# First batch of packed attention with a two-layer MoE: order of loads, weight conversion and products

## Chip, cores and metric

One core of a Trainium2 chip runs the whole program. The metric is device microseconds of one execution. The engines are named PE (TensorE, matrix products; PEld is its weight load), DVE (VectorE), ACT (ScalarE), POOL (GpSimd) and SP (SyncE, which issues all DMAs here).

## The reference, cut to what matters

```python
batch, n_heads, seq, head_dim = (8, 8, 576, 64); n_pack = 32
def sm_attn(qq, kk, vv):
    s = scale * np.matmul(qq, kk.transpose(0, 1, 3, 2))
    s = s - np.max(s, axis=-1, keepdims=True)
    a = np.exp(s)
    a = a / (np.sum(a, axis=-1, keepdims=True) + 1e-09)
    return np.matmul(a, vv)
p_packed = sm_attn(p, k, v)
out = sm_attn(q, p_packed, p_packed)
x = out, heads side by side            # 4608 tokens x 512
h = x @ w_in;  g = np.maximum(0.01 * h, h);  x = g @ w_out        # first layer, d_ff 2048
h = x @ w_in2; g = h / (1 + np.exp(-1.702 * h)); out = g @ w_out2 # second layer
```

The attention inputs are single precision. The four weights come as double precision, and the kernel reads them as pairs of 32-bit words.

## The kernel before, in words

There are four stages: attention together with the first layer's input product (batch by batch, about the first quarter of the span), the first output product, the second input product, and the second output product. The change is in the first stage only, and in it in batch 0 and in the steps of batch 1 that are prepared during batch 0.

**A batch.** `s1` (L221) makes the scores of packed queries against keys, their maxima on DVE and their exponentials on ACT. `packed` (L251) transposes the exponentials on PE, copies them on ACT and DVE, multiplies by the values, scales, and leaves the packed result in `ppk` (L284). `s2` (L286) exists for two halves of 288 tokens: scores of the queries against `ppk` on PE, a 32x32 transpose on DVE (L296), maximum and difference (L299, L300), exponential on ACT (L302), sum, reciprocal and scaling (L305 to L308), transpose back (L313), a rounded high part on ACT (L315) and the low part on DVE (L317). `prod_m` (L319) multiplies `ppk` with one chunk of 512 columns of the converted `w_in1` (four chunks c = 0 to 3), and splits the result into a high part (ACT, L325) and a low part (DVE, L327). `l1` (L331) is the main product: one unit is one block of 128 output columns for one half, six matmuls (L338), then the leaky unit on ACT (L343), which frees the PSUM bank (three such banks). A batch has 32 units; units 0 to 7 use chunk 0, 8 to 15 chunk 1, 16 to 23 chunk 2, 24 to 31 chunk 3. After each fourth call on a pair of blocks SP stores the result.

**Conversion.** `w_in1` is converted during batch 0 alone. `load_w1(c)` issues four DMAs of 512 KB (L365) into eight rotating buffers, so chunk c+2 overwrites chunk c. `w1_piece(c, k)` converts one of the four pieces of a chunk in `to_f32` (L115): two ACT operations (L121, L122), then two DVE operations (L125, L128), then one addition on POOL (L129). The scratch tile that L122 writes and L129 reads has four copies, one for each k, so chunk c+1's piece k may write it only when the addition of chunk c's piece k has ended. A product of chunk c needs all four pieces.

**Order.** Every engine executes its own instructions in program order. Up to the first unit the order is written out by hand (L377 to L404). After that, unit n is followed by `side(n)`, which issues what has been put on the agenda for that step by `at` and `pieces`; each `next` of a generator issues the work up to its next `yield`, and `run(piece, n)` does n of these. In the kernel before, chunk 0 is converted inside the first half's softmax, units 0 to 3 follow on the first half, then units 4 to 7 on the second; chunks 1, 2 and 3 are converted at steps 0 to 4, 8 to 12 and 16 to 20, each piece with ACT at one step and DVE and POOL at the next, and their products stand at steps 5, 13 and 21. Batch 1's `s1`, `packed` and the two `s2` stand at steps 8 to 12, 14 to 21, 22 to 29 and 24 to 31, its first product at 26 to 29, and batch 2's `s1` begins at step 29.

**PSUM.** Scores, transposes and products share five rotating banks under one tag (`aux`), so a late release of one holds up whatever comes five allocations later.

Of the kernel before, what the change touches and what calls it, by code (L numbers as in the profile page):

```python
# [46 lines left out]
def packed_attention_moe_moe_kernel(tc, qT, kT, vm, vt, pT, w_in1, w_out1, w_in2, w_out2, out):  # L47
# [32 lines left out]
    with ExitStack() as ctx:  # L80
# [10 lines left out]
        def at(step, *todo):  # L91
            agenda.setdefault(step, []).extend(todo)
# [16 lines left out]
        def pieces(piece, steps):  # L109

            for step in steps:
                at(step, lambda: next(piece, None))
# [73 lines left out]
        def aux(name):  # L186
            return ps.tile([P, 512], F32, tag="aux", name=name, bufs=5)

        def load_p(b):
            tp[b] = px.tile([P, H, J], F32, tag="p", name=f"p_{b}")  # L190
            nc.sync.dma_start(tp[b], pT[b])

        def load_k(b):
            tk[b] = px.tile([P, 2, 2, S], F32, tag="k", name=f"k_{b}")
            for g in range(2):
                nc.sync.dma_start(tk[b][:, g], kT[b, g])
# [7 lines left out]
        def load_q(b):  # L204
            tq[b] = px.tile([P, 2, 4, TH], F32, tag="q", name=f"q_{b}")
            for hf in range(2):
                nc.sync.dma_start(tq[b][:, hf], qT[b, hf])
# [13 lines left out]
        def s1(b):  # L221
            k, p = tk.pop(b), tp.pop(b)
            t = [[None, None], [None, None]]
            for hf in range(2):
                for par in range(2):
                    t[par][hf] = aux(f"s1_{b}_{par}_{hf}")
                both([t[0][hf], t[1][hf]], lambda r, i, par: p[r, 2 * i + par, :],
                     lambda r, i: k[r, i // 2, i % 2, hf * TH:hf * TH + TH], TH)
            if b:
                after(load_k, b + 1)  # L230
                after(load_p, b + 1)
            yield
            mx, sm = (px.tile([P, 2, 2], F32, tag=w, name=f"{w}_{b}") for w in ("mx", "sm"))
            nb, r = (px.tile([P, 2], F32, tag=w, name=f"{w}_{b}", bufs=2) for w in ("nb", "r"))
            e = px.tile([P, 2, S], F32, tag="e", name=f"e_{b}")
            e1[b] = e, r
            for par in range(2):
                for hf in range(2):
                    nc.vector.reduce_max(mx[:, par, hf:hf + 1], t[par][hf][:, :TH], axis=AX.X)
                nc.vector.tensor_scalar(nb[:, par:par + 1], mx[:, par, 0:1], mx[:, par, 1:2], -SCALE, op0=ALU.max, op1=ALU.mult)  # L240
                yield
            for par in range(2):
                for hf in range(2):
                    nc.scalar.activation(e[:, par, hf * TH:hf * TH + TH], t[par][hf][:, :TH], AF.Exp, bias=nb[:, par:par + 1],
                                         scale=SCALE, accum_out=sm[:, par, hf:hf + 1])
                yield
            for par in range(2):
                nc.vector.tensor_scalar(r[:, par:par + 1], sm[:, par, 0:1], sm[:, par, 1:2], 1e-9, op0=ALU.add, op1=ALU.add)
            nc.vector.reciprocal(r, r)

        def packed(b):  # L251

            e, r = e1.pop(b)
            et = px.tile([P, 2, 5, P], F32, tag="et", name=f"et_{b}")
            rest = aux(f"tr_{b}")
            for par in range(2):
                t = aux(f"t1_{b}_{par}")
                for k in range(4):
                    nc.tensor.transpose(t[:, P * k:P * k + P], e[:, par, P * k:P * k + P], ident)
                nc.tensor.transpose(rest[:64, P * par:P * par + P], e[:, par, 512:576], ident)  # L260
                yield
                nc.scalar.copy(et[:, par, 0:4, :], t.rearrange("p (k n) -> p k n", k=4))
            nc.vector.tensor_copy(et[:64, :, 4, :], rest[:64, :2 * P].rearrange("p (a n) -> p a n", a=2))
            yield
            v = tv.pop(b)
            o = px.tile([P, 2, D], F32, tag="o", name=f"o_{b}")
            for par in range(2):
                t = aux(f"pp_{b}_{par}")
                for k in range(5):
                    n = P if k < 4 else 64  # L270
                    for i in range(4):
                        c0 = D * (2 * (i % 2) + par)
                        nc.tensor.matmul(t[32 * i:32 * i + 32, :D], lhsT=et[:n, par, k, 32 * i:32 * i + 32],  # L273
                                         rhs=v[:n, i // 2, k, c0:c0 + D], start=(k == 0), stop=(k == 4))
                if par and b:
                    after(load_v, b + 1)
                yield
                nc.vector.tensor_scalar(o[:, par, :], t[:, :D], r[:, par:par + 1], None, op0=ALU.mult)
            yield
            t = aux(f"t2_{b}")  # L280
            nc.tensor.transpose(t[:, :P], o.rearrange("p a d -> p (a d)"), ident)
            yield
            ppk[b] = px.tile([P, 4, J], F32, tag="ppk", name=f"ppk_{b}", bufs=2)
            nc.scalar.copy(ppk[b], t[:, :P].rearrange("p (i j) -> p i j", i=4))  # L284
# [66 lines left out]
        def warm(n):  # L351

            for _ in range(n):
                nc.tensor.matmul(keep[:, :P], lhsT=ident, rhs=ident, start=True, stop=True)
# [4 lines left out]
        raw1 = {}  # L359

        def load_w1(c):
            for k in range(4):
                n = (4 * c + k) % 8
                raw1[c, k] = room[:, 1024 * n:1024 * n + 1024]
                nc.sync.dma_start(raw1[c, k], w_in1_v[:, k, 1024 * c:1024 * c + 1024])  # L365

        def w1_piece(c, k):
            v = room[:, 8192 + 512 * (k % 4):8704 + 512 * (k % 4)].bitcast(F32)
            yield from to_f32(w1[:, k, 512 * c:512 * c + 512], raw1[c, k].rearrange("p (w t) -> p w t", t=2), v)

        def run(piece, n=99):
            for _ in range(n):
                if next(piece, 0) == 0:
                    break


        load_p(0)  # L377
        load_k(0)
        load_v(0)
        load_q(0)  # L380
        load_w1(0)
        load_w1(1)
        warm(20)
        run(s1(0))
        load_k(1)
        load_p(1)
        warm(8)
        run(packed(0))
        load_v(1)
        halves = [s2(0, hf) for hf in range(2)]  # L390
        next(halves[0])
        next(halves[1])
        load_q(1)
        w1p = [w1_piece(0, k) for k in range(4)]
        next(halves[0])
        for k in range(4):
            next(w1p[k])
            if k < 3:
                next(halves[0])
            next(w1p[k])  # L400
        run(halves[0])
        m0 = prod_m(0, 0)
        run(m0)
        load_w1(2)  # L404
        pieces(halves[1], (0, 0, 0, 1, 2, 2, 3))
        at(5, lambda: load_w1(3))
        for c in range(1, 4):
            for k in range(4):
                s = 8 * c - 8 + k
                at(s, lambda c=c, k=k: raw1.update({("p", c, k): w1_piece(c, k)}))  # L410
                at(s, lambda c=c, k=k: next(raw1["p", c, k]))
                at(s + 1, lambda c=c, k=k: next(raw1["p", c, k]))
            pieces(prod_m(0, c), (8 * c - 3, 8 * c - 3, 8 * c - 2, 8 * c - 1))
        for b in range(B):
            s = 32 * b
            if b + 1 < B:
                if b == 0:
                    first, second = (8, 9, 9, 10, 11, 12), range(14, 22)
                    third, fourth = range(22, 30), range(24, 32)
                else:  # L420
                    first, second = (-3, -2, -2, 0, 1, 2), range(5, 13)
                    third, fourth = ([k + i for k in (0, 1, 2, 4, 5, 7, 10, 11)] for i in (13, 17))
                for piece, when in ((s1(b + 1), first), (packed(b + 1), second), (s2(b + 1, 0), third),
                                    (s2(b + 1, 1), fourth), (prod_m(b + 1, 0), range(26, 30))):
                    pieces(piece, [s + k for k in when])
            if b:
                for c in range(1, 4):
                    pieces(prod_m(b, c), [s + 8 * c - 6 + k for k in range(4)])
# [110 lines left out]
        for k in range(EARLY):  # L539
            s = 32 * (B - 2) + 20 + 8 * k  # L540
# [182 lines left out]
        for q in range(2):  # L723
            s = 14 * NJ * q
# [3 lines left out]
        for k in range(EARLY):  # L728
            s = 7 * (4 * NJ + 2 * k + 2)
# [82 lines left out]
```

## Time and profile before

| | |
|---|---|
| median of 3 runs | 1481.79 us (1481.16 to 1482.88) |
| the profiled execution's own time | 1488.2 us |
| its span | 1486.4 us |
| busy: PE, DVE, ACT, POOL | 95%, 75%, 56%, 7% of the span |
| mean granted PE clock | 0.98 of full speed |

The span is the time from the first to the last instruction of the profiled execution. Busy shares are means over stages with different limits. Stretches are given in microseconds from the span's start. In a list of instructions in order of time the columns are start, duration, engine, line, operation, tile written and tiles read, shapes, count, and in brackets the engine's idle time before it with what ended it. In a list of groups they are the count, the busy time and the mean of one in ns, and the idle time before with what ended it.

### The profile page before, as it was taken

Reading aid. Unit: us, or ns where it says so; the run is one execution under the profiler, and the core shown is the slowest. Engines: PE = TensorE matmul, PEld = TensorE weight load, DVE = VectorE, ACT = ScalarE, POOL = GpSimd, SP = SyncE. Lnnn points to the kernel's source line nnn. Section 1 sums busy time; section 2 is a strip of 40 time slices with the busy share of each in tenths; the row PEclk is TensorE's granted clock in tenths of the full one; section 3 lists DMA queues with packets and bytes.
Section 4 is the critical chain, followed back from the end, with each engine's and each line's share of the span. In section 5 each row is a group of like instructions: output and inputs, shape, how many; then the busy total and the mean of one; then the engine's idle time right before and its main releaser. Section 6 shows DMA issues by size and latency. Waiting matters only on the chain.

```text
span 1486.4 us, 27714 instructions
## 1 busy us (share of the span) xinstructions
PE 1417.2 (95%) x10400; PEld 1322.9 (89%) x10400; DVE 1107.5 (75%) x2068; ACT 836.2 (56%) x1791; POOL 100.4 (7%) x71
## 2 busy tenths in 40 slices
PE   6789999999979999999889999999999999999998
PEld 4567777778979999999789999999999999999998
DVE  5667777762859888888987887877648877777776
ACT  3656666665435545555656766666645655445443
POOL 1311110100001010110100010000000000000000
PEclk8889999999989999999999999999999999999999
DMA  9459999969993655635357786786768524515421
GB/s 365 159 194 318 308 325 307 335 212 337 325 301 118 212 187 164 223 105 197 120 184 249 250 282 238 244 276 204 242 216 276 170 88 148 181 54 170 129 85 43
DMA packets 228773, 317.42 MB, mean 214 GB/s; under 512 B 12576, under 2 KB 188704, under 8 KB 228640
## 3 DMA queue, kind: packets, MB, share of 16 engines
q1 hardware_dynamic: 228640, 315.67, 63.9%
q8 instruction: 81, 1.33, 0.4%
q14 instruction: 52, 0.43, 0.1%
HBM read 191.89 MB, written 123.73 MB: 212 GB/s over the span
## 4 chain that ended last, share of the span: by engine, by line
PE 71%; DVE 17%; issue 4%; DMA 3%; ACT 2%; POOL 2%; SPq 1%; DVEq 0%; ACTq 0%; POOLq 0%
PE sum L762 23%; PE h L684 20%; PE y L650 14%; PE h L338 10%; DVE ba L107 3%; PE m L218 2%; POOL b_wi L129 1%; PE pp L273 1%; PE s L218 1%; DVE m L327 1%; DVE br L482 1%; DVE br L484 1%; DVE wj L107 1%; DVE ya L107 1%; DVE da L107 1%
## 5 line engine op out<-in xcount | busy, mean ns | idle before, releaser
L684 PE MATMUL h<-ya,wj 128*128 128x384 f32 x2016 | 357.7, 338 | 6.7 <-DVE uv L692 2.4
L684 PEld LDWEIGHTS h<-ya,wj 128*128 128x128 f32 x2016 | 352.5, 189 | 11.7 <-DVE uv L692 4.1
L338 PEld LDWEIGHTS h<-a,m 128*128 128x128 f32 x1536 | 215.7, 195 | 53.7 <-ACT g L343 22.1
L650 PE MATMUL y<-ba,wo 128*128 128x384 f32 x1296 | 238.1, 341 | 19.6 <-DVE ba L107 10.9
L650 PEld LDWEIGHTS y<-ba,wo 128*128 128x128 f32 x1296 | 225.6, 189 | 31.2 <-DVE ba L107 22.4
L492 ACT CAST ba<-br 128x384 fp32r<-128x384 f32 x336 | 164.5, 513 | 149.7 <-PE y L650 89.8
L338 PE MATMUL h<-a,m 128*128 128x288 f32 x1536 | 239.5, 309 | 9.3 <-ACT a L315 3.5
L492 ACT CAST da<-dr 128x384 fp32r<-128x384 f32 x336 | 166.3, 514 | 145.2 <-PE sum L762 105.4
L762 PE MATMUL sum<-wo,da 128*128 128x256 f32 x1944 | 232.4, 281 | 1.6 <-DVE da L107 1.4
L762 PEld LDWEIGHTS sum<-wo,da 128*128 128x128 f32 x1944 | 230.2, 188 | 3.2 <-DVE da L107 3.2
L107 DVE TENSOR_TENSOR da<-dr,da 128x384 fp32r<-128x384 f32 x336 | 172.8, 554 | 40.5 <-ACT da L492 40.4
L107 DVE TENSOR_TENSOR ba<-br,ba 128x384 fp32r<-128x384 f32 x336 | 175.7, 556 | 25.5 <-ACT ba L492 25.5
L343 ACT ACTIVATE g<-h 128x288 f32<-128x288 f32 x256 | 105.2, 416 | 99.7 <-PE h L338 98.0
L762 PE MATMUL sum<-wo_early,da 128*128 128x256 f32 x1080 | 132.4, 285 | 1.7 <-ACT da L492 1.6
L762 PEld LDWEIGHTS sum<-wo_early,da 128*128 128x128 f32 x1080 | 131.5, 193 | 2.2 <-ACT da L492 1.9
L650 PE MATMUL y<-ba,wo_early 128*128 128x384 f32 x720 | 128.2, 340 | 2.3 <-ACT ba L492 2.2
L650 PEld LDWEIGHTS y<-ba,wo_early 128*128 128x128 f32 x720 | 126.4, 190 | 3.3 <-ACT ba L492 2.4
L327 DVE TENSOR_TENSOR m<-m,m 128x512 fp32r<-128x512 f32 x64 | 43.0, 684 | 54.6 <-ACT m L325 54.2
L129 POOL TENSOR_TENSOR b_wo<-v_wo,b_wo 128x512 int32<-128x512 int32 x32 | 42.5, 1330 | 485.5 <-DVE v_wo L128 367.6
L677 ACT ACTIVATE g<-cc 128x384 f32<-128x384 f32 x96 | 50.4, 525 | 31.6 <-DVE cc L700 27.1
L107 DVE TENSOR_TENSOR wj<-wjs,wj 128x512 fp32r<-128x512 f32 x88 | 55.8, 647 | 9.7 <-ACT wj L626 9.7
L692 DVE TENSOR_TENSOR uv<-uv,h 128x384 f32<-128x384 f32 x48 | 26.5, 553 | 46.5 <-PE h L684 39.9
(114 smaller groups left out, 1372.1 us busy)
## 6 DMA issues: line engine op xcount, KB each, us to landing
g_scratch<-g SPq DMA_DIRECT2D x64, 576.0 KB, 5.3
br<-g_scratch SPq DMA_DIRECT2D x96, 384.0 KB, 7.0
g_scratch<-g SPq DMA_DIRECT2D x96, 384.0 KB, 5.4
dr<-g_scratch SPq DMA_DIRECT2D x96, 384.0 KB, 4.3
wjs<-wi_scratch SPq DMA_DIRECT2D x22, 896.0 KB, 5.8
wo_scratch<-hl_wo SPq DMA_DIRECT2D x32, 448.0 KB, 6.0
wo<-wo_scratch SPq DMA_DIRECT2D x27, 512.0 KB, 8.9
k<-in_kT_dram SPq DMA_DIRECT2D x16, 576.0 KB, 6.3
```

The lines of the kernel that those rows point to most:

```text
L107: at(step + 1, lambda: nc.vector.tensor_sub(*rest))
L129: nc.gpsimd.tensor_tensor(d, v.bitcast(I32), d, op=ALU.add)
L218: nc.tensor.matmul(tiles[par][32 * i:32 * i + 32, :n], lhsT=lhsT(r, i, par), rhs=rhs(r, i), start=True, stop=True)
L327: nc.vector.tensor_sub(m[:, 1, par, :], t[par], m[:, 0, par, :].bitcast(F32))
L338: nc.tensor.matmul(t[:, :TH], lhsT=m[:, ws, par, o:o + P], rhs=a[:, xs, par, :], start=(k == 0), stop=(k == 5))
L343: nc.scalar.activation(g1t[g][:, f % 2, hf * TH:hf * TH + TH], t[:, :TH], AF.Prelu, alpha=0.01)
L492: nc.scalar.copy(t[:, 0, :], src)
L650: nc.tensor.matmul(acc[BANK[p]][:, c, :HB], lhsT=w[:, ws, P * c:P * c + P], rhs=x[:, xs, :], start=(p in OPENS and f + m == 0), stop=(f == ...
L677: nc.scalar.activation(g[f][:, HB * i:HB * i + HB], src, AF.Gelu_apprx_sigmoid)
L684: nc.tensor.matmul(b, lhsT=w[:, ws, c, P * kk:P * kk + P], rhs=x[:, xs, kk, :], start=(p in OPENS and kk + s == 0), stop=(kk + s == 3), sk ...
L692: nc.vector.tensor_add(v, v, b)
L762: nc.tensor.matmul(b, lhsT=x[:, xs, P * c:P * c + P], rhs=w[:, ws, :], start=(p in OPENS and f == 0 and m == 0 and c != 1), stop=(f == NJ ...
```

## The change

`load_w1(0)` is issued in front of the keys, values and queries. Three of chunk 0's four pieces are converted while the keys are still to be used, the fourth between the two copies of the transposed exponentials. Both halves' score products and the whole product of chunk 0 are issued one after another, and the second half's softmax is interleaved with the first's, down to two last pieces. The ACT part of a piece is issued a chunk ahead of its DVE and POOL parts: chunk 1's before unit 0, chunk 2's at steps 1 to 4, chunk 3's at steps 6 to 9; the DVE and POOL parts stand at steps 0 to 3, 5 to 8 and 10 to 13. The products of chunks 1, 2, 3 move to steps 4, 9 and 15. Batch 1's `s1`, `packed` and two `s2` move to steps 5 to 9, 11 to 15, 16 to 23 and 18 to 25. `load_w1(2)` goes in front of batch 1's keys; `load_w1(3)` and batch 1's queries are loaded at step 4.

```diff
--- before.py
+++ after.py
@@ -375,48 +375,47 @@
 
 
         load_p(0)
+        load_w1(0)
         load_k(0)
         load_v(0)
         load_q(0)
-        load_w1(0)
         load_w1(1)
         warm(20)
-        run(s1(0))
+        w1p = [w1_piece(c, k) for c in range(4) for k in range(4)]
+        sc, pk = s1(0), packed(0)
+        run(sc, 1)
+        warm(8)
+        for k in range(3):
+            run(w1p[k], 2)
+        run(sc)
+        run(pk, 2)
+        run(w1p[3], 2)
+        run(pk)
+        halves = [s2(0, hf) for hf in range(2)]
+        load_w1(2)
         load_k(1)
         load_p(1)
-        warm(8)
-        run(packed(0))
         load_v(1)
-        halves = [s2(0, hf) for hf in range(2)]
-        next(halves[0])
-        next(halves[1])
-        load_q(1)
-        w1p = [w1_piece(0, k) for k in range(4)]
-        next(halves[0])
-        for k in range(4):
-            next(w1p[k])
-            if k < 3:
-                next(halves[0])
-            next(w1p[k])
-        run(halves[0])
+        h0, h1 = halves
         m0 = prod_m(0, 0)
-        run(m0)
-        load_w1(2)
-        pieces(halves[1], (0, 0, 0, 1, 2, 2, 3))
-        at(5, lambda: load_w1(3))
-        for c in range(1, 4):
-            for k in range(4):
-                s = 8 * c - 8 + k
-                at(s, lambda c=c, k=k: raw1.update({("p", c, k): w1_piece(c, k)}))
-                at(s, lambda c=c, k=k: next(raw1["p", c, k]))
-                at(s + 1, lambda c=c, k=k: next(raw1["p", c, k]))
-            pieces(prod_m(0, c), (8 * c - 3, 8 * c - 3, 8 * c - 2, 8 * c - 1))
+        for piece, n in ((h0, 1), (h1, 1), (m0, 1), (h0, 3), (m0, 1), (w1p[4], 1), (h1, 2), (m0, 1), (h0, 2), (h1, 1),
+                         (m0, 9), (h0, 9), (w1p[5], 1), (h1, 2), (w1p[6], 1), (w1p[7], 1)):
+            run(piece, n)
+        pieces(h1, (0, 1))
+        for n in range(4, 16):
+            s = 5 * (n // 4) - 5 + n % 4
+            at(s, lambda n=n: run(w1p[n], 1))
+            if n < 12:
+                at(s + 1, lambda n=n: run(w1p[n + 4], 1))
+        at(4, lambda: load_w1(3), lambda: load_q(1))
+        for c, when in ((1, (4, 4, 5, 6)), (2, (9, 9, 10, 11)), (3, (15, 15, 16, 17))):
+            pieces(prod_m(0, c), when)
         for b in range(B):
             s = 32 * b
             if b + 1 < B:
                 if b == 0:
-                    first, second = (8, 9, 9, 10, 11, 12), range(14, 22)
-                    third, fourth = range(22, 30), range(24, 32)
+                    first, second = (5, 6, 7, 7, 8, 9), (11, 11, 12, 12, 13, 14, 14, 15)
+                    third, fourth = range(16, 24), range(18, 26)
                 else:
                     first, second = (-3, -2, -2, 0, 1, 2), range(5, 13)
                     third, fourth = ([k + i for k in (0, 1, 2, 4, 5, 7, 10, 11)] for i in (13, 17))
```

## Rows read from the trace of the kernel before

**Rows 1.** Busy PE time of L338 by stretch: length, busy (count), clock, DMA, GB/s.

```profile
32.50:69.20 36.70, 19.15 (x96) 0.80 0.53 196
69.20:99.85 30.65, 16.95 (x96) 0.86 0.52 174
99.85:138.95 39.10, 29.95 (x194) 0.98 0.86 283
...
258.95:297.95 39.00, 29.14 (x195) 1.00 1.01 335
```

**Rows 2.** Waits in the stretch 30 to 100: who waited for whom, us, times, longest.

```profile
PEld m L218 <- POOL w L129: 10.7, 7, 1.9
PEld s L218 <- DVE m L327: 3.1, 1, 3.1
```

**Rows 3.** Instructions in order of time, 0 to 34: scores, packed result, first half, first unit.

```profile
9.09 1.20 PE L218 MATMUL s<-k,p 64*32 64x288 f32 x32
...
16.25 0.27 ACT L284 COPY ppk<-t 128x128 f32<-128x128 f32 x1 [1.92 <-PE t L281]
...
17.38 0.85 DVE L296 STREAM_TRANSPOSE wf<-s 128x288 f32<-128x288 f32 x2 [1.54 <-PE s L218]
...
19.05 0.76 DVE L300 TENSOR_TENSOR wf<-wf,s2m 128x576 f32<-128x576 f32 x1
...
32.52 5.51 PE L338 MATMUL h<-a,m 128*128 128x288 f32 x24 [0.66 <-ACT m L325]
```

**Rows 4.** The two first key loads: issue, and time from issue to landing.

```profile
L196 SPq DMA_DIRECT2D k<-in_kT_dram x2: 415/420/424, 1.2 to 1.7; - x2
...
DMA to landing us min/median/max: 4.1/4.6/5.1
```

**Rows 5.** Busy (count) of PE, PEld, DVE, ACT, POOL by stretch; clock, DMA, GB/s.

```profile
16.57:32.50 15.93, 8.00 (x48) 1.19 (x48) 12.32 (x20) 6.40 (x12) 5.14 (x4) 0.71 1.03 389
32.50:69.20 36.70, 28.71 (x168) 19.48 (x169) 24.69 (x42) 20.21 (x47) 10.71 (x8) 0.80 0.53 196
69.20:99.85 30.65, 25.62 (x278) 18.11 (x276) 22.86 (x44) 15.80 (x35) 5.58 (x4) 0.86 0.52 174
```

**Rows 6.** Groups of instructions on ACT and DVE in batch 0, 32.5 to 99.85.

```profile
L121 ACT ACTIVATE w<-raw 128x512 int32<-128x512 uint32 x12 | 8.1, 676 | 0.0
...
L128 DVE SCALAR_TENSOR_TENSOR raw<-raw 128x512 uint32<-128x512 uint32 x12 | 13.1, 1088 | 0.4
L125 DVE TENSOR_SCALAR raw<-raw 128x512 uint32<-128x512 uint32 x12 | 7.3, 609 | 4.8 <-ACT raw L122 4.8
L327 DVE TENSOR_TENSOR m<-m,m 128x512 fp32r<-128x512 f32 x10 | 6.8, 686 | 14.2 <-ACT m L325 14.2
L239 DVE TENSOR_REDUCE mx<-s 128x1 f32<-128x288 f32 x8 | 3.2, 447 | 0.0
...
L317 DVE TENSOR_TENSOR a<-a,a 128x576 fp32r<-128x576 f32 x3 | 2.3, 753 | 0.1
```

**Rows 7.** Busy time of what touches tile wf, both halves of one batch's second softmax.

```profile
99.85:138.95 39.10, 9.26 (x16) 1.36 (x2) 0.98 0.86 283
```

**Rows 8.** POOL in order of time: two additions of chunk 2.

```profile
60.83 1.31 POOL L129 TENSOR_TENSOR w<-raw,w 128x512 int32<-128x512 int32 x1 [0.70 <-ACT e L244]
62.84 1.26 POOL L129 TENSOR_TENSOR w<-raw,w 128x512 int32<-128x512 int32 x1 [0.69 <-DVE r L248]
```

**Rows 9.** DVE in order of time, 57 to 64: L128 beside no addition, and during one.

```profile
57.97 0.69 DVE L128 SCALAR_TENSOR_TENSOR raw<-raw 128x512 uint32<-128x512 uint32 x1
58.58 0.43 DVE L125 TENSOR_SCALAR raw<-raw 128x512 uint32<-128x512 uint32 x1
59.05 1.64 DVE L128 SCALAR_TENSOR_TENSOR raw<-raw 128x512 uint32<-128x512 uint32 x1
```

**Rows 10.** PE in order of time: one unit at granted clock 0.5, one at 1.0.

```profile
66.01 1.75 PE L338 MATMUL h<-a,m 128*128 128x288 f32 x6
...
68.06 1.04 PE L338 MATMUL h<-a,m 128*128 128x288 f32 x6
```

## The prediction

> **What bounds the kernel now.** I read the busy time of the main product by stretch first. Every middle batch takes 39.0 or 39.1 us, but batch 0's 32 units take 36.70 + 30.65 = 67.35 us at 0.80 and 0.86 of the clock, and they start only at 32.52 [rows 1, 3]. So batch 0 costs 28 us more than a middle batch, and that excess is all the change can win there. The waits say why: PE waits 10.7 us for POOL's additions, in front of the chunk products, and 3.1 us for one DVE difference that holds a PSUM bank [rows 2]. DVE is busy 24.69 of 36.70 and 22.86 of 30.65 us, POOL 10.71 and 5.58 [rows 5]: no engine is full, so the loss is in the order, three engines following each other while PE stands in its queue in front of a product. In the middle batches PE works on the main product for about 29 to 30 of 39 us, and its other products fill most of the rest; there is nothing of this change there.
>
> I follow four points: `ppk`, the first unit, unit 16, and batch 1's first unit, at 16.5, 32.5, 69.2 and 99.85 us in the trace.
>
> **The front.** The four word loads (2.10 MB) go in front of the keys. The last keys landed at 1.7 + 5.1 = 6.8 us [rows 4], and the loads move 389 GB/s when the queue is full [rows 5], so the words delay the keys by 2.10/0.389 = 5.4 us, to 12.2. The scores started at 9.09, behind the warming matmuls, not behind the keys [rows 3], so only part of it shows: most of the scores wait for the second group of keys, which leaves about 0.9 of their 1.2 us after 12.2. They end at about 13 instead of 10.3: +2.6. The values and queries behind it land later by as much, still ahead of their use. Three word pieces are converted in this wait; a piece costs ACT two operations of 0.676 = 1.35 us [rows 6], DVE 0.43 + 0.69 = 1.12 alone [rows 9], POOL about 1.3 [rows 8]. They land from about 5.3 us on, where the first keys landed (1.2 + 4.1) [rows 4], so ACT, DVE and POOL are through before the maxima begin; I cost them at nothing, and if the words came 4 us later the exponentials would queue behind them. The fourth piece stands on ACT between the two copies of `packed`, and on DVE in front of its copy: 1.35 + 1.12 = 2.5 us, of which I take 1.7, since part of it lies beside the transposes. So `ppk` ends at 16.5 + 2.6 + 1.7 = 20.8, later than before by 4.3.
>
> Then both score products and chunk 0's whole product run on PE without a wait. Before, four pieces sat inside the first half's softmax. Now the chain is: 0.8 to the first transposed scores [rows 3], the first half's DVE work on `wf`, 9.26/2 = 4.63 [rows 7], about 0.45 of short operations (an estimate, from the gap between sum and scaling), the second half's beginning (0.85 and two of 0.76) 2.4 put between (the exponential runs beside it) [rows 3], one difference of the product 0.69, the high part 0.67 on ACT (an estimate: as an L121), and the low part 0.75 [rows 6]: 10.4. The first unit with all its operands is at about 31.3, say 31.5, against 32.5: **-1.0**.
>
> **Units 0 to 15.** ACT first does three pieces of chunk 1 (4 us) in front of unit 0's evacuation, so with three banks PE stops after three units until about 35.4. Nobody else is hurt: DVE is on the second half until 35.1 (2.9 us from 32.2). What sets this stretch is the conversion of chunks 1, 2 and 3. Additions follow each other by 62.84 - 60.83 = 2.01 us when DVE keeps up [rows 8]: the addition of 1.3 and L128's 0.69 don't overlap, as L128 takes 1.64 when it starts during an addition [rows 9]. Chunk 1 then starts at 35.1, gives 1.1 us to the second half's low part, and ends its last addition at about 44; its product (step 4) at 45. PE stands idle there for 5 us or so, as before. For the remaining eight pieces I sum DVE: 8 x 1.70 = 13.6 (13.1 + 7.3 over 12 pieces, blocking included) [rows 6], four differences 2.7, batch 1's maxima 1.8 [rows 6] and about 1.3 of short operations (an estimate): 19.4, plus 2 us for ACT, which between 49 and 59 has chunk 3's four pieces (5.4), four exponentials, copies and evacuations in one queue. That ends chunk 3 at about 65.5 and its product at 66. Units 0 to 15 thus take 34.5 us instead of 36.7: **-2.2**, although they now hold all three chunks instead of two.
>
> **Units 16 to 31.** Nothing of the conversion is left. In it are the two second softmaxes of batch 1 (DVE about 12), chunk 3's and batch 1's first splits (2.8) and 16 units. This is the mix of a middle batch, 39.1 for 32 units [rows 1]; half is 19.55, and I take 19.8. Against 30.65: **-10.9**. The 3.1 us wait for the bank goes too, since the softmaxes end at step 25 and no longer meet the next scores at step 29.
>
> **Moved loads.** SP holds chunk 2's words until chunk 0's buffers are read (by 18 us, when the queue is still full); batch 1's keys and values land behind them by about 35 and are wanted at step 5, about 46. Chunk 3's words and batch 1's queries wait at step 4 on SP for chunk 1's L128; behind them stands the first store, which only becomes ready at step 5. The words land by about 47, and ACT wants the first at 49. I cost these at nothing. DMA was busy 0.53 and 0.52 of batch 0 [rows 1].
>
> **Sum.** -1.0 - 2.2 - 10.9 = -14.1 us: batch 1 starts at about 85.8. The later batches and stages run by steps and only move forward. The profiled execution has a span of 1486.4 us and a time of 1488.2, 6.4 above the median of the runs; taking 14 from the median, 1481.8, gives 1467.8.
>
> **Unknown costs.** The pace of a piece isn't shown for this order. Below, DVE alone, 1.12; above, one piece after another on three engines, 1.35 + 1.12 + 1.3 = 3.8; I take 2.01, the row of two neighbouring additions. The word loads' delay lies between 5.4 (389 GB/s) and 10.7 us (half that rate, 196 GB/s, of rows 5); I take the full queue's rate, which it is here. At its best (DVE not blocked, 12 x 0.58 = 7 us less) the gain is 21; with the slow loads 5 us of it go.
>
> **Rivals.** *The clock.* A unit's six matmuls take 1.75 us at clock 0.5 and 1.04 at full speed [rows 10]. PE still stands idle in front of unit 0 and of chunk 1's product, and has short gaps until chunk 3. If half clock lasts into units 16 to 23, 8 x 0.71 = 5.7 us are lost: 1473.5. For it: batch 0 had 0.86 in its second half [rows 1]. Against: that half had gaps of its own, which go. The Trainium skill, TensorE: Matmul & The Clock Gate, section Why this matters for your kernels, warns against idle stretches between bursts of matmuls because the clock drops to half; by that rule the two long gaps that the new order keeps would slow what follows them. The trace agrees in kind: 0.71 in the front after `ppk`, where PE had 8.00 of 15.93 us [rows 5].
>
> *The pipeline is serial (slower).* If ACT, in order, must wait with L122 for the addition four pieces back, evacuations queue behind it, PE stops, and DVE waits for ACT in turn, a piece costs up to 3.8 us in units 0 to 15: 12 x (3.8 - 2.0) = 21 us more, 1489. It decides from 3.2 us a piece on, where the 14 us are gone (14/12 = 1.2 above 2.0). For it: ACT carries everything in steps 5 to 9. Against: four scratch copies let ACT be a whole chunk ahead, and neighbouring additions came at 2.0 with less lead.
>
> *Taken back.* DMA is 0.86 to 1.01 busy in the middle batches [rows 1]. If loads set their pace, an earlier start could be eaten: 1481.8. Against: DMA has half its time free in batch 0, and the batches don't lengthen with the DMA share (39.1 us at 0.86, 39.0 at 1.01).
>
> **Numbers.** Forecast 0.64, clock 0.18, taken back 0.08, serial 0.10. A change of 0.2% (3 us) is about what a measurement tells from none. Faster 0.82, same 0.08, slower 0.10. The range, 1460.5 to 1478, runs from the best pace (21 us) to a gain of 4, where the clock's loss and slow loads together leave hardly more, and leaves out the last two cases.
>
> **What would show it.** In the changed profile: scores ending near 13, `ppk` near 21, first unit near 31.5; additions of a chunk about 2 us apart, last one near 65; unit 16 near 66 and batch 1's first unit near 86; no PE wait on DVE's difference at the end of batch 0; middle batches still about 39 us. I am wrong if additions come over 3 us apart, if the first unit is later than 36, or if middle batches grow.

## The result, and the profile after

The changed kernel takes 1470.68 us (median of 4 runs, 1469.54 to 1472.50), the kernel before 1482.34 beside it (1481.16 to 1487.93). The medians differ by 11.7 us; the ratio of the runs, 0.9904 with a 95% interval of 0.9874 to 0.9934, is worth about 14, and two repeats below (a1 and a2) give medians 14.5 and 16.9 us apart. The profiled execution took 1471.63 us, its span is 1469.8 against 1486.4; the execution profiled of the kernel before was slower than its median, so the runs' times, not the two spans, give the gain.

Main product on PE by stretch, as in [rows 1] (length, busy and count, clock, DMA share, GB/s):

```profile
32.05:67.30 35.25, 17.04 (x96) 0.93 0.65 218
67.30:86.95 19.65, 14.45 (x96) 1.00 0.68 220
86.95:125.30 38.35, 29.22 (x194) 1.00 0.90 302
125.30:164.90 39.60, 29.28 (x194) 1.00 0.99 317
243.90:282.75 38.85, 29.01 (x194) 1.00 1.01 336
```

The first half of batch 0 takes 35.25 us instead of 36.70, the second 19.65 instead of 30.65. Batch 1 starts at 87.0 instead of 99.9, and the middle batches don't grow: the 39.60 us of the batch from 125.30 on stand against 39.60 of the same batch before, which [rows 1] leaves out.

The front in order of time, as in [rows 3]:

```profile
10.71 0.69 PE L218 MATMUL s<-k,p 64*32 64x288 f32 x8 [1.42 <-DMA k<-in_kT_dram]
12.05 1.17 PE L218 MATMUL s<-k,p 64*32 64x288 f32 x24 [0.66 <-DMA k<-in_kT_dram]
...
19.30 1.30 PE L273 MATMUL pp<-v,et 64*32 64x64 f32 x48 [1.99 <-DVE et L263]
...
21.52 0.27 ACT L284 COPY ppk<-t 128x128 f32<-128x128 f32 x1 [3.31 <-PE t L281]
...
32.09 0.61 PE L338 MATMUL h<-a,m 128*128 128x288 f32 x1 [6.38 <-ACT a L315]
```

The scores now wait for the keys' two landings (idle 1.42 and 0.66 us); `ppk` ends at 21.79, and PE loses 1.99 us of it to DVE's copy behind the fourth piece. The first unit comes only 0.4 us sooner.

Waits in the stretch 30 to 88, as in [rows 2]:

```profile
PEld m L218 <- POOL w L129: 8.0, 4, 2.1
...
ACT raw L122 <- POOL w L129: 3.2, 4, 1.3
...
DVE r L248 <- ACT e L244: 1.9, 1, 1.9
...
PEld s L218 <- DVE m L327: 0.2, 1, 0.2
```

The wait of batch 2's scores for a bank falls from 3.1 to 0.2 us. DVE waits nowhere for ACT's part of a piece. ACT, a chunk ahead, now waits 3.2 us in all for the addition four pieces back, which frees its scratch tile. Additions on POOL, a pair of chunk 1 and the last pair of chunk 3:

```profile
41.73 1.32 POOL L129 TENSOR_TENSOR w<-raw,w 128x512 int32<-128x512 int32 x1 [0.69 <-DVE raw L128]
43.74 1.32 POOL L129 TENSOR_TENSOR w<-raw,w 128x512 int32<-128x512 int32 x1 [0.69 <-DVE raw L128]
...
62.13 1.34 POOL L129 TENSOR_TENSOR w<-raw,w 128x512 int32<-128x512 int32 x1 [1.16 <-DVE raw L128]
64.63 1.30 POOL L129 TENSOR_TENSOR w<-raw,w 128x512 int32<-128x512 int32 x1 [1.16 <-DVE raw L128]
```

From its second piece on chunk 1 runs at 2.0 us a piece, chunk 3 at 2.5, and the last addition ends at 65.9 instead of 81.5.

### The profile page after: what moved, and what is told of

Its sections match the earlier page's. It is cut to its first block, busy times and chain, and to the rows that moved or that the text cites. A ratio compares the mean times of both kernels' runs of the same rounds, so it can differ in the third digit from the quotient of the medians.

```text
span 1469.8 us, 27704 instructions
## 1 busy us (share of the span) xinstructions
PE 1403.5 (95%) x10400; PEld 1315.9 (90%) x10400; DVE 1106.6 (75%) x2068; ACT 836.6 (57%) x1791; POOL 100.0 (7%) x71
## 4 chain that ended last, share of the span: by engine, by line
PE 69%; DVE 17%; DMA 5%; issue 3%; ACT 3%; POOL 2%; SPq 1%; DVEq 0%; ACTq 0%; POOLq 0%
PE sum L761 23%; PE h L683 19%; PE y L649 13%; PE h L338 10%; DVE ba L107 3%; PE m L218 2%; POOL b_wi L129 1%; DMA raw_wo<-in_w_out_dram 1%; PE s L218 1%; DMA br<-g_scratch 1%; DMA wo_scratch<-b_wo 1%; DMA yq<-y_scratch 1%; DVE br L481 1%; PE pp L273 1%; DVE wj L107 1%
## 5 line engine op out<-in xcount | busy, mean ns | idle before, releaser
L338 PEld LDWEIGHTS h<-a,m 128*128 128x128 f32 x1536 | 209.5, 190 | 55.3 <-ACT g L343 24.9
L649 PE MATMUL y<-ba,wo 128*128 128x384 f32 x1296 | 238.7, 341 | 16.9 <-DVE ba L107 11.9
L338 PE MATMUL h<-a,m 128*128 128x288 f32 x1536 | 232.6, 303 | 12.5 <-ACT a L315 6.4
L129 POOL TENSOR_TENSOR b_wo<-v_wo,b_wo 128x512 int32<-128x512 int32 x32 | 42.6, 1331 | 485.4 <-DVE v_wo L128 381.0
L676 ACT ACTIVATE g<-cc 128x384 f32<-128x384 f32 x96 | 50.4, 525 | 31.8 <-DVE cc L699 27.3
```

Source lines behind the costliest of these rows:

```text
L129: nc.gpsimd.tensor_tensor(d, v.bitcast(I32), d, op=ALU.add)
L338: nc.tensor.matmul(t[:, :TH], lhsT=m[:, ws, par, o:o + P], rhs=a[:, xs, par, :], start=(k == 0), stop=(k == 5))
L649: nc.tensor.matmul(acc[BANK[p]][:, c, :HB], lhsT=w[:, ws, P * c:P * c + P], rhs=x[:, xs, :], start=(p in OPENS and f + m == 0), stop=(f == ...
L676: nc.scalar.activation(g[f][:, HB * i:HB * i + HB], src, AF.Gelu_apprx_sigmoid)
```

## The experiments

All edits start from the changed kernel, except the run `e9_lead_alone`. Times of the kernel before differ from chip to chip (medians 1482 to 1489 us), so ratios are compared. The points, in us of each profile (`ppk` ends, a unit starts; unit 16 is the first of the second half):

| run | `ppk` | unit 0 | last addition starts | unit 16 | batch 1 | ratio to before (95%) |
|---|---|---|---|---|---|---|
| before | 16.5 | 32.5 | 80.3 | 69.4 | 99.9 | 1 |
| changed | 21.8 | 32.1 | 64.6 | 67.3 | 87.0 | 0.9904 (0.9874 to 0.9934) |
| a1, changed again | 23.0 | 33.3 | 67.3 | 70.0 | 89.7 | 0.9900 (0.9883 to 0.9917) |
| a2, a third time | 21.6 | 31.8 | 64.7 | 68.9 | 88.6 | 0.9883 (0.9866 to 0.9899) |
| e1, front before | 16.4 | 32.4 | 68.7 | 72.8 | 92.5 | 0.9940 (0.9919 to 0.9961) |
| e2, batch 1's steps before | 22.5 | 32.8 | 62.8 | 60.8 | 89.0 | 0.9913 (0.9898 to 0.9928) |
| e3, no lead | 22.4 | 32.8 | 80.0 | 82.4 | 102.0 | 0.9992 (0.9980 to 1.0005) |
| e4, no additions | 21.4 | 31.3 | none | 64.1 | 83.8 | one run, 1469.52 us |
| e5, warmed gap | 21.8 | 32.1 | 64.6 | 68.8 | 88.4 | 0.9914 (0.9895 to 0.9932) |
| e6, fourth piece later | 19.2 | 29.0 | 61.5 | 65.6 | 85.3 | 0.9893 (0.9868 to 0.9918) |
| e7, more later | 19.6 | 29.4 | 61.2 | 65.0 | 84.7 | 0.9890 (0.9872 to 0.9908) |
| e10, as e7 again | 19.9 | 29.7 | 61.4 | 65.3 | 84.9 | 0.9877 (0.9862 to 0.9892) |
| e8, spread | 19.5 | 29.4 | 61.9 | 66.1 | 87.7 | 0.9906 (0.9892 to 0.9919) |
| e9, lead alone | 17.1 | 33.1 | 76.6 | 68.2 | 95.8 | 0.9962 (0.9949 to 0.9976) |

The three profiles of the changed kernel show how little one profile can tell: they spread by 2.7 us at batch 1's first unit.

**ACT's lead (e3).**

```diff
-            at(s, lambda n=n: run(w1p[n], 1))
-            if n < 12:
-                at(s + 1, lambda n=n: run(w1p[n + 4], 1))
+            at(s, lambda n=n: run(w1p[n], 2))
```

(and the four ACT parts in front of unit 0 left to steps 0 to 3.)

> The ACT part of each piece of chunks 1 to 3 is issued in the same step as its DVE and POOL parts instead of a chunk ahead; all else as changed. Theory: DVE and POOL set the pace, and ACT has time; unit 0 is evacuated 4 us sooner, but in each step DVE waits for ACT's 1.35 us behind an evacuation, of which a part is hidden by other DVE work: batch 1's first unit 2 to 5 us later, at 89 to 92, 1472 to 1476 us. Rival one (the lead is what makes the gain): each of 12 pieces costs 1.35 us more on the path, batch 1's first unit at 103, about 1486 us. Rival two (the lead gives nothing): 87, 1470.7 us.

Rival one's number holds: 102.0, and the ratio cannot be told from 1. My theory fell here, and the profile shows why; it also shows that the cost is not 1.35 us at each piece, as the rival had it. In order of time, chunk 1's last addition and what follows, in e3:

```profile
46.35 1.26 POOL L129 TENSOR_TENSOR w<-raw,w 128x512 int32<-128x512 int32 x1 [0.70 <-DVE raw L128]
49.17 1.06 PE L338 MATMUL h<-a,m 128*128 128x288 f32 x6
...
50.27 0.41 ACT L343 ACTIVATE g<-h 128x288 f32<-128x288 f32 x1 [0.41 <-PE h L338]
50.58 0.66 ACT L121 ACTIVATE w<-raw 128x512 int32<-128x512 uint32 x1
...
51.82 0.43 DVE L125 TENSOR_SCALAR raw<-raw 128x512 uint32<-128x512 uint32 x1 [5.61 <-ACT raw L122]
...
53.12 1.27 POOL L129 TENSOR_TENSOR w<-raw,w 128x512 int32<-128x512 int32 x1 [5.51 <-DVE raw L128]
```

Chunk 2's first ACT part stands behind unit 5's evacuation, that behind unit 5 on PE, that behind chunk 1's product, and that behind chunk 1's last addition. So the conversion of a chunk can't start before the product of the chunk ahead of it, and 6.8 us pass between two additions that are 2.0 apart with the lead. Over all twelve, additions start 3.7 us apart, against 2.5 in the changed kernel. In this run's waits between 32 and 103:

```profile
DVE raw L125 <- ACT raw L122: 19.9, 6, 5.6
```

DVE waits 19.9 us for ACT's part, in six waits of up to 5.6; in the changed kernel this wait is not in the list. One limit of this run: the kernel before issued ACT's part one step ahead, and e3 takes that step away too. Whether the new steps need a lead of a whole chunk, or one step would do, was not tried.

**The lead alone (e9).** The kernel before with this in place of its conversion steps, and chunk 1's ACT parts in front of unit 0:

```diff
-                s = 8 * c - 8 + k
...
+                s = 8 * c - 7 + k
+                at(s, lambda n=4 * c + k: run(w1p[n], 1))
+                if c < 3:
+                    at(s + 1, lambda n=4 * c + k + 4: run(w1p[n], 1))
```

> The kernel before with one edit: the ACT part of the pieces of chunks 1 to 3 is issued a chunk ahead, chunk 1's before the first unit; loads, front, products and batch 1's steps as before. Theory (ACT's lead is the larger part of the gain, since it takes ACT's place in the step out of the path from one chunk's product to the next chunk's conversion): batch 1's first unit at 93 to 96 instead of 99.9, 0.995 to 0.997 of the kernel before. Rival (lead and earlier steps gain only together): 98 to 101.

95.8, and 0.9962: the lead alone gives 4.1 us in the profile. The earlier steps without any lead (e3) give nothing, both together 10 to 13. So moving the steps up pays only with ACT's parts out of them.

**The front (e1).** The hand-written front of before, then chunk 1's ACT parts, then the second half at steps 0 to 3.

> The front as in the kernel before (keys first, chunk 0 converted inside the first half's softmax, the second half's softmax left to steps 0 to 3); the conversion of chunks 1 to 3 and batch 1's steps as changed. Theory: the first unit hardly moves (32.1 in the changed kernel, 32.5 before), but the second half's softmax, about 5 us of DVE work, and chunk 1's four ACT parts now stand in front of chunk 1's DVE parts, so everything behind shifts: unit 16 near 72, batch 1's first unit near 92, about 1476 us against 1470.7. Rival (the front gives only the 0.4 us of its first unit, and the agenda all the rest): batch 1's first unit near 87.5, about 1471 us.

92.5 and 0.9940: the theory's numbers. The first unit is at 32.4, inside the 31.8 to 33.3 of the changed kernel; the front's worth, 2.8 to 5.5 us against its three profiles, is what is done by then.

**Batch 1's steps (e2).** `first, second = (8, 9, 9, 10, 11, 12), range(14, 22)`, `third, fourth = range(22, 30), range(24, 32)`, products at steps 5, 13 and 21.

> The front and the conversion steps as changed; the products of chunks 1 to 3 at steps 5, 13 and 21 and batch 1's scores, packed result and second softmaxes at their steps of before. Theory: the conversion ends sooner, since DVE has less between its pieces (last addition near 60), but batch 1's preparation crowds into the last units again, and the wait for a PSUM bank at step 29 comes back with some 3 us: unit 16 near 62 to 64, batch 1's first unit near 90 to 91, about 1474 us. Rival (the conversion alone decides): batch 1's first unit at 85 to 87, 1469 to 1471 us.

89.0 in the profile. The wait for the bank came back at its old length, in the stretch 60 to 90 of e2:

```profile
PEld s L218 <- DVE m L327: 3.1, 1, 3.1
```

But unit 16 came at 60.8, 6.5 us sooner than in the changed kernel, so what the last units lost the first had gained. The total is inside the spread of the three profiles above and the ratio is not apart from the changed kernel's: what batch 1's steps are worth stays open.

**The additions (e4).** POOL's L129 left out for chunks 1 to 3: `if add:` in front of it.

> Leaves out POOL's additions of chunks 1 to 3, so the output is not the layer's; all else as changed. Theory (the addition and DVE's second operation exclude each other and set the pace of a piece): L128 always takes 0.69, neighbouring pieces are 1.1 us apart where DVE has nothing else, units 0 to 15 shorten by 5 to 7 us, batch 1's first unit at 80 to 82. Rival (ACT sets the pace in units 0 to 15): L128 shortens, but batch 1's first unit moves by less than 2 us.

DVE's two operations in e4's first 16 units, and the same two in the changed kernel's batch 0:

```profile
L128 DVE SCALAR_TENSOR_TENSOR raw<-raw 128x512 uint32<-128x512 uint32 x12 | 8.3, 695 | 0.4
L125 DVE TENSOR_SCALAR raw<-raw 128x512 uint32<-128x512 uint32 x12 | 5.0, 417 | 0.0
```

```profile
L128 DVE SCALAR_TENSOR_TENSOR raw<-raw 128x512 uint32<-128x512 uint32 x12 | 11.2, 930 | 0.4
L125 DVE TENSOR_SCALAR raw<-raw 128x512 uint32<-128x512 uint32 x12 | 8.6, 717 | 0.0
```

Blocking costs DVE 19.8 - 13.3 = 6.5 us, close to the prediction's 7. The Trainium skill, SBUF — State Buffer, section Who interferes with whom, says that a DVE instruction with two SBUF inputs, as L128 is, contends with a GpSimd instruction that reads SBUF, and that `tensor_scalar`, as L125 is, can take the shared ports in its two-port modes. This run agrees: with the additions gone both operations run at their undisturbed length. The path, however, shortens by only 3.2 us against the first profile of the changed kernel (4.8 and 5.9 against its repeats), between the theory and the rival. In its last part PE was at half clock in this run (units 10 to 15; engines' busy time in e4's stretch, clock behind POOL's column), so how much the additions alone are worth is not separated from the clock:

```profile
53.00:64.00 11.00, 8.30 (x115) 6.47 (x115) 4.74 (x11) 3.12 (x8) 0.00 (x0) 0.69 0.47 155
```

**The clock (e5).** `warm(10)` behind chunk 0's product.

> The changed kernel with ten more warming matmuls on PE behind chunk 0's product, where PE stood idle for 6.4 us in front of the first unit. Theory: the granted clock falls later or less there (0.5 from 20 to 37 us in the changed kernel) and the first units take about 0.85 us instead of 1.7, but DVE and POOL set the pace up to unit 16, so batch 1's first unit stays within 0.5 us of 87.0 and the time within 1 us of the changed kernel's. Rival (half clock in the front is paid for in full): 2 to 3 us less, batch 1's first unit at 84 to 85.

The twelve additions start within 0.03 us of the changed kernel's, although from 20.0 to 37.1 us the mean granted clock is 0.80 instead of 0.50. So half clock between chunk 0's product and the first units costs the conversion nothing, which is what it would do if DVE and POOL set that pace. But unit 16 came 1.4 us later, as the clock fell once more, late, and batch 1's first unit at 88.4, outside the theory's 0.5 us and away from the rival's side. The stretch 62.8 to 66.2 of e5, then of the changed kernel:

```profile
62.80:66.20 3.40, 3.40 (x48) 2.79 (x48) 2.12 (x4) 0.41 (x1) 1.92 (x2) 0.50 0.02 5
```

```profile
62.80:66.20 3.40, 3.40 (x59) 3.01 (x58) 2.04 (x4) 0.83 (x2) 1.97 (x2) 1.00 0.18 25
```

**Towards a better order (e6, e7, e8, and the changed kernel beside them).**

```diff
-        run(pk, 2)
-        run(w1p[3], 2)
-        run(pk)
+        run(pk, 4)
+        run(w1p[3], 1)
+        run(pk, 2)
+        run(w1p[3], 1)
+        run(pk)
```

> The changed kernel with chunk 0's fourth piece moved behind the copies of the transposed exponentials: its ACT part behind the first product with the values, its DVE and POOL parts behind the second scaling. Theory: the packed result is ready 1.3 to 1.7 us sooner (near 20.3 instead of 21.8), and everything behind it comes sooner by that: first unit near 30.7, batch 1's first unit near 85.6. Rival (the values' or queries' landing, or the conversion's pace, holds the front): packed result sooner by less than 0.5, or sooner without effect on unit 16.

`ppk` 2.6 us sooner, the first unit 3.1, the last addition 3.2, batch 1 only 1.7. Around the last addition the clock was at 0.50, from 59.6 to 63.0 us, as late as in e5.

e7 has that edit, chunks 1 and 2 split at `(4, 4, 6, 7)` and `(9, 9, 11, 12)`, and batch 1's scores at `(5, 6, 7, 7, 8, 12)`.

> As the run before it, and two of DVE's waits taken out of its queue between pieces: the splits of chunk 1's and 2's products one step later, and batch 1's sums of exponentials at step 12 instead of 9, where DVE stood idle 1.2 and 1.9 us for ACT. Theory (any idle moment of DVE between pieces is lost time): 2 to 3 us less on top, batch 1's first unit near 83, about 3.5 to 4.5 us below the changed kernel. Rival (ACT, which is busy 24 of 35 us there, takes DVE's place as the bound): less than 1 us on top of the run before it.

The rival's number: 0.6 us on top, but not by the rival's route over ACT. From the first to the last addition's start DVE is idle 2.1 us here and 4.0 in e6, and busy 25.0 against 23.7: with the pieces closer together, its two operations on them, which the additions lengthen (e4), take 19.8 us instead of 18.7. In e6 between these points, then in e7:

```profile
L128 DVE SCALAR_TENSOR_TENSOR raw<-raw 128x512 uint32<-128x512 uint32 x11 | 10.5, 952 | 0.4
L125 DVE TENSOR_SCALAR raw<-raw 128x512 uint32<-128x512 uint32 x11 | 8.2, 746 | 0.0
```

```profile
L128 DVE SCALAR_TENSOR_TENSOR raw<-raw 128x512 uint32<-128x512 uint32 x11 | 13.3, 1212 | 0.4
L125 DVE TENSOR_SCALAR raw<-raw 128x512 uint32<-128x512 uint32 x11 | 6.5, 591 | 0.0
```

e8 also moves chunk 2's and 3's products to steps 11 and 18, batch 1's packed result and softmaxes by two steps, and has its sums at step 11.

> The changed kernel with the fourth piece later, as in the run of that edit, and PE's own order loosened: the products of chunks 2 and 3 at steps 11 and 18 instead of 9 and 15, batch 1's packed result at steps 13 to 17, its second softmaxes at 18 to 25 and 20 to 27. Theory (with the front shortened, units 8 to 15 wait on PE for products that nobody wants yet): unit 16 at 62 to 64, batch 1's first unit at 83 to 84.5, 2 to 4 us below the changed kernel. Rival (the softmaxes, now later, meet batch 2's scores at step 29): unit 16 sooner, but batch 1's first unit not before 85.3.

The rival: unit 16 sooner, batch 1 at 87.7, and a ratio like the changed kernel's.

> The changed kernel once more, beside the two below on one chip: 12 to 15 us below the kernel before, batch 1's first unit at 87.0 again.

Batch 1 at 89.7, not 87.0; the medians 14.5 us apart, as expected. So I took the changed kernel and e7's edit once more, side by side.

> The changed kernel a third time, beside the run below on one chip. Its profile's points moved by up to 2.7 us between two profiles with the place of the granted clock's falls: batch 1's first unit is expected at 86.5 to 90.

> The kernel with the fourth piece, the splits and the sums later, beside the changed kernel. If its earlier points (84.7 for batch 1's first unit, against 87.0) are the order's and not the clock's, its median is 2 to 4 us below the changed kernel's on this chip, and the ratio to the kernel before 0.987 to 0.989; rival (the clock's falls set the difference): within 1 us of the changed kernel.

Batch 1 at 88.6 and at 84.9. e7's two profiles (84.7, 84.9) lie below all three of the changed kernel, by 2.1 us at the least, so the order seems to bring 2 us or more to that point. The medians differ by 1.3 us (1471.66 and 1470.34), between what either side expected, and the intervals overlap: a version clearly faster than the changed kernel is not shown. Part of e7's lead is gone again by batch 4: batch 3 takes 1.35 us longer than in the changed kernel, at a lower clock. The main product in batch 3, in e7 and then in the changed kernel (length, busy and count, clock, DMA share, GB/s):

```profile
162.65:204.05 41.40, 30.34 (x194) 0.96 0.97 317
```

```profile
164.90:204.95 40.05, 28.99 (x194) 1.00 0.97 321
```

## Why the prediction was right

*The front.* Scores to end near 13: they ended at 13.2. `ppk` at 20.8: 21.8. I took 1.7 us for the fourth piece; e6, which takes it out of that place, has `ppk` 2.6 sooner, 0.3 of it from keys that landed earlier. First unit 31.5: 32.1. The term was -1.0 and came out at -0.4.

*Units 0 to 15.* Forecast 34.5 us, measured 35.25; -2.2 against -1.45. The pace of 2.01 us held in chunk 1, but not between its first two pieces (2.84), so its last addition ended at 45.1 instead of 44. The DVE sum for the other eight pieces made up for over half of that and gave the end of chunk 3 (65.5 forecast, 65.9 measured). Chunk 3's product, 1.1 us long, then stood in front of unit 16, where the forecast had left it half a microsecond. That the blocking is in the DVE sum is shown by e4: DVE spends 19.8 us on twelve pieces with the additions (1.65 each, where I took 1.70) and 13.3 without. How much of it is on the path stays open.

*Units 16 to 31.* Forecast 19.8, measured 19.65; -10.9 against -11.0. The bank wait went as forecast. This term carried the sum, but the border between the two stretches is set by the steps: in e2 the same sixteen units take 28.2 us and units 0 to 15 take 28.0, for nearly the same total. The middle batch whose half I took is not always 39.0 or 39.1 us either: in the kernel before some took 37.5 to 40.75.

*Sum.* Batch 1 at 85.8 forecast, 87.0 measured, a gain of 12.9 of the 14 forecast. The time, 1470.68, is 2.9 above the forecast of 1467.8. The profiles' spans differ by more than 12.9 us (16.6), in part because batches behind it ran at less clock in the kernel before: batch 1 took 39.10 us at 0.98 there and 38.35 at 1.00 in the changed kernel.

*Rivals.* "Taken back" is out: the middle batches keep their 38 to 40 us. "The clock" had half clock last into units 16 to 23; in the first profile the clock was at 1.00 from 37.1 us on. The half clock in front of that cost the conversion nothing (e5). A single late fall does cost: 1.4 us at unit 16 in e5, and 1.6 in a2, where the last addition stands at 64.7 as in the first profile and the clock was at 0.50 from 62.8 to 66.2. "Serial" did not come, but e3 shows how near it was: the same steps without the lead reach 102.0, later than before. What I had put against that rival, ACT's lead, is what decides, and I had not priced it; how long a lead it takes is open.

## What to carry to other kernels

When three engines share a conversion, look at what each part stands behind in its own engine's queue, not at how busy the engine is: ACT was busy 20 of 37 us in the kernel before, and its part still held DVE up, because it stood behind an evacuation that waited for the previous chunk's product; the lead alone, on the same work, was worth 4.1 us. Issue the part with slack ahead (here a chunk), with as many scratch copies as that needs, and only then move the other steps up. One profile's points carry the clock's accidents with them: repeat the profile before reading 2 us.

## What was not expected

One kernel's profiles differ by 2.7 us at batch 1's first unit, and the places at which the clock falls in batch 0 differ with them. By stretches of 10 us from 10 to 60, the first profile of the changed kernel had 1.00, 0.50, 0.64, 1.00, 1.00, the second this:

```profile
10.00:20.00 10.00, 7.20 (x90) 5.02 (x90) 5.51 (x14) 4.22 (x12) 2.59 (x2) 0.83 1.03 383
...
30.00:40.00 10.00, 6.53 (x26) 6.22 (x27) 9.53 (x18) 6.27 (x13) 1.67 (x1) 0.50 0.55 188
40.00:50.00 10.00, 7.61 (x44) 2.91 (x51) 8.21 (x11) 6.10 (x13) 5.22 (x4) 0.84 0.76 233
```

There the clock fell early, among the first scores: 24 of their matmuls took 1.84 us instead of 1.17, and `ppk` came at 23.0 instead of 21.8. A later fall, at 0.50 from 46.8 to 50.2 us, went with the rest: the additions were 1.2 us late in front of it and 2.7 at the end. So half clock was free here in the gap behind chunk 0's product, and not where the next step waited for PE. The Trainium skill, TensorE: Matmul & The Clock Gate, section What's actually happening, says that the chip's watch on PE's activity runs freely and does not start with the kernel; falls at other places in the same kernel agree with that, and nothing here shows more.
